# Wider operations, one y product a step and a new order in an S4 convolution with a GEGLU block

## The chip, the cores and the metric

The program runs on one core of one Trainium2 chip. The metric is the device time of one execution in microseconds (us). Five engines work side by side, each through its own instructions in order: TensorE (PE, matrix products), VectorE (DVE, elementwise), ScalarE (ACT, functions from a loaded table), GpSimd (POOL) and SyncE (SP). SP, ACT and POOL also issue the DMA transfers.

## The reference, cut to what matters

```python
h = layernorm(x) * (1 + ca) + sa            # x: 2048 tokens x 448 channels, N = 256 states
dt = exp(log_dt)                            # a value for each channel
P = exp((dt * (A_re + i A_im))[:, :, None] * l)          # l = 0 .. 2047
K = Re(einsum("dn,dnl,dn->dl", C, P, dt * B))            # a filter of 2048 taps for each channel
x = x + ga * (causal_conv(K, h) + h * Dskip)             # by FFT of length 4096
h = layernorm(x) * (1 + cb) + sb
x = x + gb * ((gelu(h @ w_gate) * (h @ w_up)) @ w_down)  # 448 -> 1792 -> 448
```

The six rows sa, ca, ga, sb, cb, gb are `silu(c) @ w_mod`.

## The kernel before, in words

**Filter.** The filter is made channel group by channel group: 56 steps of 8 channels. A tap index is split in two parts, l = 64 l1 + l2, so that a complex power is a product of an "x" table (32 values of l1) and a "y" table (64 values of l2), each a magnitude times a cosine or sine. For a step, PE multiplies the prepared exponents (tile `lt`) with constants (`ea`, `rd`) into PSUM tile `pg`; ACT takes exp of it for the magnitudes (`mx`, `my`; lines 775 and 793) and sine and cosine for the phases (tile `fg`; lines 811 to 830, in two ways: for the first 28 steps the cosine gets its own PSUM tile, for the last 28 it is made from an absolute value). DVE multiplies magnitude and phase: `tx` (line 855), and `ty` in three operations (`mults`, lines 859, 862, 863: cosine half, then the sine half in two pieces, one with a factor of -1). PE sums over the states: 64 small products into `kg` (`kgen`, line 886). After every second step `ktail` copies `kg` to `ke`, adds Dskip, multiplies with a small DFT matrix (line 911) and copies to `ako`.

**Preparation.** The exponents of a tile of 112 channels are made by `prep(t)`, t = 0 to 3: C times B as a complex product (lines 658 to 667), its size (square, log, square root by exp) and angle (reciprocal, arctan), each value then split in three bf16 pieces (`pieces`: cast, subtract, cast, subtract; lines 587, 643, 649) so that bf16 products on PE keep enough digits. Results go to DRAM (`lh_d`, line 696, `put0` and `put1`) and come back rearranged as `lt` (line 751), once per 7 steps and half: `lt0` for exp, `lt1` for the angles. Its inputs arrive in three DMAs (`q<-in_abc`, line 615). A block of ones for each tile (`lh_d<-in_k_one`, line 622) is copied by POOL's queue.

**Tokens.** Meanwhile the input is normalised with rows from `w_mod` (line 950), transformed (lines 1040, 1103), and stored; blocks of frequencies are then multiplied with those of the filter and transformed back (`k_fft`, lines 1194 to 1205, for the channel groups 0 to 159 and 160 to 319; `t_fft`, lines 1276 to 1300, for the last 128, after the last step). Copies from PSUM may run on ACT or DVE (`cp`, lines 585 and 587).

**GEGLU.** Four blocks of 512 tokens follow: convolution back (lines 1466, 1471), norm, transposes, gate and up products (line 1594), down products (lines 1663, 1694).

**Order.** The program is not written in its final order. Each piece of work is a task with a name, an engine (or a choice of two) with an assumed duration, the tasks that it needs and the buffers that it takes. `Plan.order` places tasks one by one: it takes the engine that could start earliest, and among that engine's tasks that could start within 0.25 us (ACT: 0.02 us) the one with the lowest number in the table `PRIO`. The order so found is what each engine then runs, in order. The assumed durations, a hop of 0.3 us between engines (`HOP`), 1.3 us for a table (`TABLE`) and 280 KB per us of DMA (`RATE`) enter that order alone; nothing of them is on the chip.

Of the kernel before, what the change touches and what calls it, by code (L numbers as in the profile page):

```python
# [37 lines left out]
WS = 256.0  # L38
PRIO = {
    "anc": (-1293.256, -3578.895, -353.961, -872.318, -460.437, -1921.377, -2404.991, -2215.805, 191.288, -32.981, -202.691,  # L40
        -2647.333, -1933.83, -670.792, -192.873, -616.144, -80.921, -1549.964, -2941.687, -671.342, -2001.879, -1132.111,
        -71.643, -27.945, -252.965, -1535.421, -769.379, -1539.333),
    "ang": (-63.859, -7.725, -30.71, 0.169, 7.925, 11.195, 9.268, 21.779, 22.824, 25.594, 26.183, 26.493, 28.144, 28.708,
# [5 lines left out]
    "c.ai": (-2663.528,),  # L49
    "c.ak": (171.218,),  # L50
    "c.au": (-4200.533,),
    "c.c": (-933.544,),
    "c.ea": (5422.27,),
    "c.id": (-147.248,),
    "c.ih": (1109.11,),
    "c.ld": (-3220.083,),
    "c.rd": (2966.135,),
    "co.adde": (-84.218, -1452.145, -2417.83, -1409.323),
    "co.addl": (-57.786, 676.69, 1533.586, 31.466),
    "co.addx": (-1428.076, -8.045, 2531.362, 3088.204, -2578.892, 2089.375, -473.92, 382.232, 1219.977, -537.482, 53.247,  # L60
        1140.208),
    "co.c2": (553.038, 3254.154, 1888.633, -595.169, 1726.527, -906.573, 4858.759, 40.493, -1400.834, 27.831, 1819.503,
        -161.366),
    "co.h": (336.967, 2645.855, 1868.777, -2126.118),
    "co.h2": (-650.973, 75.139, 637.166, -1259.465, -8.18, -1329.599, 13.947, -1333.575, 5413.552, -346.388, 3335.76, 1270.416),
    "co.l": (-2527.984, -675.661, 723.03, 3544.242),
    "co.l2": (1124.467, 1797.664, 1246.234, 626.032, 529.696, 1269.558, 529.646, -451.738, -1181.182, 2221.273, 450.372,
        434.525),
    "co.mme": (4028.037, 3822.614, -709.965, -3597.943),
    "co.mml": (-661.981, 33.929, 1870.772, -68.779),  # L70
    "co.mmx": (348.366, -620.465, 1977.413, 2997.574, -279.998, 3308.134, 630.569, 742.671, -398.692, -288.917, -47.372,
        2601.845),
    "co.n": (-637.705, -78.904, -2172.773, -124.152),
    "co.nx": (-1207.602, 1920.968, -700.888, 0.561, -1307.228, -3639.226, 373.628, -35.065, -24.718, 34.24, 1425.966, -6133.847),
    "co.rc": (1435.224, -2102.468, 1120.167, 435.885),
    "co.rcx": (864.192, -118.249, 3179.105),
    "co.rt": (-668.81, -40.146, 1435.174, -1099.33),
    "co.rtx": (-306.185, -80.314, 5310.55),
    "co.t": (-701.977, -362.858, 11.547, -251.511),
    "co.t2": (-1003.663, 677.507, 490.748, 1973.53, -67.147, -1774.919, -292.344, -677.791, 196.69, -3024.797, -183.214, 15.548),  # L80
    "cos": (47.809, 4338.677, -1916.389, -1985.479, 48.84, 450.345, -228.642, 1373.754, -1635.183, -2125.449, -2951.945,
        139.392, -590.217, -1488.189, -465.57, -115.397, -138.704, 2366.141, 654.971, 78.486, 63.259, -3501.827, 365.129,
        -594.75, 843.446, -2481.552, 3748.658, 338.746),
    "cos2": (-186.283, -458.553, -28.501, -1467.414, -186.383, 305.735, -4173.308, 2676.943, -903.314, -2645.906, -803.054,
        147.233, 61.493, -902.839, -698.019, 3.975, 96.182, 670.288, 4882.18, -890.924, -903.013, 1267.647, -38.519, 1684.391,
        654.047, -1006.703, 490.617, -217.831),
    "d.hi": (-16.935, -885.611, 1072.565, -1866.073, 565.92, -545.207, 277.832),
    "d.ld": (-1036.334, 594.218, -5342.563, -1512.808, 784.13, 1290.275, -992.387),
    "d.lo": (-1950.133, -1401.218, -2174.946, -390.7, -1260.169, -6.416, 1957.309),
    "d0": (-1079.999,),  # L90
    "dn": (-3573.259, -323.838, 1692.909, 1720.273),
    "dn.k0": (1759.554, 521.981, -3993.33),
    "dn.k2": (-1082.302, -1650.584, -6237.94),
    "dn.k3": (-388.073, 2717.888, 2751.692),
    "dn.r": (586.912, 103.145, 2224.364, -500.948),
# [430 lines left out]
def s4_geglu(ctx: ExitStack, tc: tile.TileContext, a: dict, out: bass.AP):  # L526
# [76 lines left out]
    def prep(t):  # L603
# [32 lines left out]
        def pieces(lb, q, get, deps, k, first):  # L636
# [5 lines left out]
            def p2():  # L642
                V.tensor_sub(get(), get(), lb.tile[:, q])
# [1249 lines left out]
```

## Time and profile before

| | us |
|---|---|
| median of 3 runs (823.48 to 825.14) | 824.81 |
| the profiled execution's own time | 822.29 |
| its span, first to last instruction | 820.5 |
| busy in the span: PE | 744.8 (91%) |
| DVE | 609.2 (74%) |
| ACT | 464.4 (57%) |

The span falls in four stages: to about 45 us the start, to 371 the 56 filter steps with the transforms beside them, to 420 the last transforms and the first normalisation, and to the end the GEGLU blocks. A busy time is the union over an engine's instructions; instructions of DVE and ACT that follow each other overlap a little in the trace, so that the distance of two starts is less than the duration of one. In a timeline row stand the start, the duration, the engine (with a q: its queue, for issues of DMAs), line, operation, output and input, and in brackets how long the engine sat idle before and what it then waited for.

### The profile page before, as it was taken

Reading aid. Unit: us, or ns where it says so; the run is one execution under the profiler, and the core shown is the slowest. Engines: PE = TensorE matmul, PEld = TensorE weight load, DVE = VectorE, ACT = ScalarE, POOL = GpSimd, SP = SyncE. Lnnn points to the kernel's source line nnn. Section 1 sums busy time; section 2 is a strip of 40 time slices with the busy share of each in tenths; the row PEclk is TensorE's granted clock in tenths of the full one; section 3 lists DMA queues with packets and bytes.
Section 4 is the critical chain, followed back from the end, with each engine's and each line's share of the span. In section 5 each row is a group of like instructions: output and inputs, shape, how many; then the busy total and the mean of one; then the engine's idle time right before and its main releaser. Section 6 shows DMA issues by size and latency. Waiting matters only on the chain.

```text
span 820.5 us, 19136 instructions
## 1 busy us (share of the span) xinstructions
PE 744.8 (91%) x8172; PEld 455.8 (56%) x8172; DVE 609.2 (74%) x1034; ACT 464.4 (57%) x610; POOL 11.1 (1%) x28
## 2 busy tenths in 40 slices
PE   0787788989899999988689999999999999999997
PEld 0333344443577766678566445444496445954477
DVE  5799999898989999996875783178884655744552
ACT  4598998999899999880245551034332233223320
POOL 1000000000000000001200000000000000000000
PEclk9879999999999999999879999999999999999999
DMA  9644459997967755989769641644416232012101
GB/s 266 161 147 138 116 145 246 282 261 234 221 198 223 224 160 165 295 276 279 242 224 310 234 158 63 162 150 139 135 53 185 77 127 96 24 68 90 45 13 35
DMA packets 92839, 136.78 MB, mean 167 GB/s; under 512 B 22672, under 2 KB 75184, under 8 KB 92754
## 3 DMA queue, kind: packets, MB, share of 16 engines
q1 hardware_dynamic: 86480, 131.02, 52.6%
q10 hardware_dynamic: 5458, 3.12, 1.3%
q8 instruction: 64, 1.05, 0.5%
q0 software_dynamic: 816, 1.42, 0.5%
q14 instruction: 21, 0.17, 0.1%
HBM read 100.42 MB, written 36.01 MB: 166 GB/s over the span
## 4 chain that ended last, share of the span: by engine, by line
PE 62%; ACT 14%; DVE 9%; DMA 8%; issue 5%; SPq 2%; ACTq 0%; DVEq 0%
PE pq L1594 30%; PE pq L1694 8%; PE pd L1663 4%; ACT fg L819 3%; PE kg L886 3%; DMA u_d<-so 2%; PE pg L806 2%; ACT my L793 2%; PE pq L1588 2%; PE pf L1205 2%; PE pf L1103 2%; PE pd L1694 1%; DMA fg<-in_w_mod 1%; DVE ty L859 1%; ACT fg L811 1%
## 5 line engine op out<-in xcount | busy, mean ns | idle before, releaser
L1594 PE MATMUL pq<-ht,wr 128*128 128x512 f16 (+1 forms) x1200 | 248.7, 365 | 0.0
L1594 PEld LDWEIGHTS <-wr 128*128 128x128 f16 x1200 | 114.4, 98 | 128.9 <-issue 12.3
L1608 DVE TENSOR_TENSOR fq<-ge,pq 128x512 f32<-128x512 f32 (+1 forms) x60 | 39.0, 651 | 83.4 <-PE pq L1594 58.5
L1601 ACT ACTIVATE ge<-pq 128x512 f32<-128x512 f32 (+1 forms) x60 | 34.0, 567 | 113.8 <-PE pq L1588 69.4
L1620 ACT ACTIVATE hh<-fq 128x1024 f16<-128x1024 f32 (+1 forms) x49 | 47.2, 964 | 59.9 <-DVE fq L1608 44.5
L886 PE MATMUL kg<-ty,tx 128*32 128x64 f32 x3584 | 63.6, 224 | 13.4 <-DVE ty L863 9.0
L886 PEld LDWEIGHTS kg<-ty,tx 128*32 128x32 f32 x3584 | 54.4, 112 | 32.7 <-DVE ty L863 14.0
L855 DVE TENSOR_TENSOR tx<-mx,fg 128x1024 f32<-128x1024 f32 x56 | 67.3, 1215 | 2.8 <-ACT fg L830 2.8
L1694 PE MATMUL pq<-d,hh 128*128 128x224 f16 x476 | 69.3, 259 | 0.0
L859 DVE TENSOR_TENSOR ty<-my,fg 128x1024 f32<-128x1024 f32 x56 | 67.9, 1216 | 1.7 <-ACT fg L823 1.7
L1694 PE MATMUL pq<-d,hlo 128*128 128x224 f16 x238 | 61.6, 259 | 0.0
L819 ACT ACTIVATE fg<-pg 128x1024 f32<-128x1024 f32 x56 | 57.7, 1032 | 3.5 <-issue 1.5
L793 ACT ACTIVATE my<-pg 128x1024 f32<-128x1024 f32 x56 | 55.9, 1037 | 5.6 <-PE pg L788 5.1
L1623 DVE TENSOR_TENSOR hlo<-fq,hh 128x1024 f16<-128x1024 f32 (+1 forms) x49 | 53.6, 1103 | 3.1 <-ACT hh L1620 3.1
L1694 PEld LDWEIGHTS <-hh 128*128 128x128 f16 x560 | 53.9, 98 | 0.8 <-issue 0.3
L1205 PE MATMUL pf<-q,fc 128*128 128x160 f32 x264 | 41.8, 307 | 0.2
L806 PEld LDWEIGHTS <-lt 64*128 64x128 bf16 x336 | 19.3, 94 | 40.0 <-issue 26.0
L1205 PEld LDWEIGHTS pf<-q,fc 128*128 128x128 f32 x264 | 36.6, 190 | 6.2 <-issue 3.4
L806 PE MATMUL pg<-ea,lt 64*128 64x512 bf16 x168 | 33.1, 387 | 6.7 <-ACT fg L819 5.2
L863 DVE TENSOR_TENSOR ty<-my,fg 128x512 f32<-128x512 f32 x56 | 38.2, 682 | 0.0
L862 DVE SCALAR_TENSOR_TENSOR ty<-my,fg 128x512 f32<-128x512 f32 x56 | 38.1, 681 | 0.0
L911 PE MATMUL kg<-ak,ke 128*64 128x128 f32 x448 | 30.6, 279 | 3.7 <-issue 2.0
(198 smaller groups left out, 1207.2 us busy)
## 6 DMA issues: line engine op xcount, KB each, us to landing
wr<-w_d SPq DMA_DIRECT2D x21, 896.0 KB, 4.6
fc<-in_k_fc SPq DMA_DIRECT2D x20, 576.0 KB, 5.2
u_d<-so SPq DMA_DIRECT2D x32, 224.0 KB, 4.5
w<-in_wgu SPq DMA_DIRECT2D x14, 512.0 KB, 4.1
ui<-u_d SPq DMA_DIRECT2D x10, 672.0 KB, 6.2
w_d<-wr SPq DMA_DIRECT2D x7, 896.0 KB, 7.1
fq<-in_wd SPq DMA_DIRECT2D x14, 448.0 KB, 3.8
us<-uo SPq DMA_DIRECT2D x22, 240.0 KB, 6.5
```

The costliest lines, as they stand in the source:

```text
L793: A.activation(yb.tile.rearrange("p a b c -> p (a b c)"), pb.tile, AF.Exp)
L806: T.matmul(pa[:, nh * 512:nh * 512 + 512], w, x, start=(k == 0), stop=(k == 2))
L819: A.activation(fb.tile[:, 0].rearrange("p x (n k) -> p n x k", n=2), pb.tile.rearrange("p (n x k) -> p n x k", n=2, x=2), AF.Sin, scale=TW ...
L855: V.tensor_mul(tx.tile, xb.tile[:, xm, None, :].to_broadcast([128, 2, 512]), fb.tile[:, :, 0])
L859: V.tensor_mul(ty.tile[:, 1], yb.tile, fy()[:, 1, :, None, :].to_broadcast([128, 16, 2, 32]))
L886: T.matmul(kg[32 * g:32 * g + 32, 2 * (s % 2) + q, :64], tx[:, r, nh, 4 * q + g], ty[:, r, nh, 4 * q + g], start=(r == 0 and nh == 0), sto ...
L1205: T.matmul(pz.tile[:, e % 32 - sl0], fc.tile[:, i, 1 + t], pp.tile[:, t, i], start=(t == 0 and e != 32), stop=(t == 1 and e != 0))
L1594: T.matmul(pb.tile[k][:, ts], wr.tile[:, 4 * lo + t, k, c0:c0 + 128], ht[:, m, ts], start=f % 2 == 0 and i == 0, stop=f % 2 == 1 and i == 9)
L1608: V.tensor_mul(to if half is None else to[:, half:half + 1], *src)
L1620: A.activation(hg.tile[0][:, cb, c], fq.tile[:, c], AF.Copy)
L1623: V.tensor_sub(hg.tile[1][:, cb, c], fq.tile[:, c], hg.tile[0][:, cb, c])
L1694: T.matmul(bank(k)[:, m], x[:, p, q[0], ts], w[:, p, q[1]], start=new and m == 0 and p == 0 and z == 0, skip_group_check=True, stop=i in ( ...
```

## The change

- **Preparation**: the inputs of a tile come in two DMAs (C and B together, then A) instead of three; the four products of C and B are one operation of 1024 columns; both values of a pair are split in pieces together (512 columns instead of 256 twice); small multiplications are folded elsewhere (`G1`).
- **Constants**: the blocks of ones of tiles 1 to 3 are read on SP's queue, each after its tile's inputs, instead of on POOL's at the start. `A_log_dt`, `c` and `A_Dskip` are laid out by the host so that a DMA reads whole rows.
- **y product**: signs move into the constants' phases (`ea`) and into the cosine's scale, and `ty` becomes one DVE operation of 2048 columns that needs sine, cosine and exp; `kgen` picks its operands from it by a stride. `my` is written in another layout.
- **Order**: assumed durations come from a table of measured ones (`COST`), hops from a table by pairs of engines, DMA is modelled by queue, PE's clock by a window; some kinds of tasks must keep their turn (`INTURN`); all numbers in `PRIO` are new.

The diff, cut:

```diff
+COST = {
+    ("anc", "PE", 0.76): 0.72, ("ang", "PE", 0.76): 0.72, ("bn", "DVE", 0.65): 0.73, ("c.ai", "SP", 0.42): 1.27,
...
 PRIO = {
-    "anc": (-1293.256, -3578.895, -353.961, -872.318, -460.437, -1921.377, -2404.991, -2215.805, 191.288, -32.981, -202.691,
...
 class Plan:
-    TABLE, HOP, STICK, BIAS, RATE = 1.3, 0.3, 103.13, -0.27, 280.0
+    TABLE, HOP, STICK, BIAS, RATE = 1.3, 0.3, 103.13, -0.27, 290.0
+    HOPD, HOPB, WINDOW, COLD, WARM, PHASE = 0.2, 0.16, 3.4133, 0.55, 0.83, 0.0
+    HOPS = {("PE", "ACT"): 0.18, ("PE", "DVE"): 0.18, ("ACT", "DVE"): 0.18, ("ACT", "PE"): 0.2, ("DVE", "ACT"): 0.115, ("DVE", "PE"): 0.14,
+            ("DVE", "DVE"): 0.12, ("ACT", "ACT"): 0.18, ("PE", "PE"): 0.0}
+    INTURN = ("ang", "tx", "tyc", "x.mm", "y.mm", "x.exp", "y.exp", "f.ut", "f.fc", "f.fwd", "f.inv", "lt0", "lt1", "ub.u", "ub.fc", "ub",
+              "kev", "ka", "t.fwd", "t.inv", "wr.ld")
...
     def prep(t):
-        for i in range(3):
-            loads.append(add("p.ld", {"SP" if i % 2 or t else "ACT": 0.42 if i % 2 or t else 0.1}, v0, lambda i=i: ld1(i), loads[:1],
-                             [b1, b2, b3] if i == 0 else [], [b1, b2, b3] if i else [], kb=253))
-
-        PAD[t] = add("pad", {"POOL": 1.0}, v0 + 0.5, lambda: P.dma_start(lh_d[t, :, :, 6:], a["k_one"][t]), loads, kb=229)
+        L0 = add("p.ld", {"SP" if t else "ACT": 0.42 if t else 0.1}, v0, lambda: ld1(0), (), us, (), kb=459)
+        PAD[t] = add("pad", {"SP": 0.7} if t else {"POOL": 1.0}, v0 + 0.5, lambda: (dma if t else P.dma_start)(lh_d[t, :, :, 6:], a["k_one"][t]), [L0], kb=300)
+        L1 = add("p.ld", {"SP": 0.42}, v0, lambda: ld1(1), [L0], (), us, kb=230)
...
-            V.tensor_mul(x, cr, br)
-            V.tensor_mul(t1, ci, bi)
-            V.tensor_sub(x, x, t1)
...
+            V.tensor_mul(b2.tile.rearrange("p (i j) n -> p i j n", i=2), b1.tile[:, :2, None].to_broadcast([DT, 2, 2, N]),
+                         b1.tile[:, None, 2:].to_broadcast([DT, 2, 2, N]))
...
     def mults(s):
-            V.tensor_mul(ty.tile[:, 1], yb.tile, fy()[:, 1, :, None, :].to_broadcast([128, 16, 2, 32]))
-
-        def fs():
-            V.scalar_tensor_tensor(ty.tile[:, 0, :, 0], yb.tile[:, :, 0], -1.0, fy()[:, 0], op0=OP.mult, op1=OP.mult)
-            V.tensor_mul(ty.tile[:, 0, :, 1], yb.tile[:, :, 1], fy()[:, 0])
+        def fy():
+            ty.tile = tab.tile([128, 2, 2, 512], FT, name="ty")
+            V.tensor_mul(ty.tile, yb.tile[:, :, None, :].to_broadcast([128, 2, 2, 512]),
+                         fb.tile[:, None, :, 1].to_broadcast([128, 2, 2, 512]))
         x = add("tx", {"DVE": 1.13}, s - 0.4, fx, [si, co, xt_], [tx], [fb, xb])
-        y = add("tyc", {"DVE": 1.13}, s - 0.4, fc_, [co, yt_], [ty], [fb, yb])
-        z = add("tys", {"DVE": 1.2}, s - 0.4, fs, [si, y], (), [fb, yb, ty])
-        return x, y, z
+        y = add("tyc", {"DVE": 2.21}, s - 0.4, fy, [si, co, yt_], [ty], [fb, yb])
+        return x, y
...
     def kgen(s, deps):
-                                     ty[:, r, nh, 4 * q + g], start=(r == 0 and nh == 0), stop=(r == 1 and nh == 1),
+                                     ty[:, 0:4:3, nh, 4 * q + g] if r else ty[:, 1:3, nh, 4 * q + g], start=(r == 0 and nh == 0), stop=(r == 1 and nh == 1),
```

Three places of the new order follow. The first is DVE's beginning. Before, the rows of tile 0's complex product (lines 658 to 667), behind a cast of the first piece:

```order
L587 CAST lh<-q 112x256
L658 TENSOR_TENSOR q<-q 112x256
L659 TENSOR_TENSOR q<-q 112x256
L660 TENSOR_TENSOR q<-q 112x256
L665 TENSOR_TENSOR q<-q 112x256
L666 TENSOR_TENSOR q<-q 112x256
L667 TENSOR_TENSOR q<-q 112x256
L643 TENSOR_TENSOR q<-q,lh 112x256
```

The same beginning now; L727 is the product of 1024 columns, L732 and L733 the two sums, L741 to L744 the size:

```order
L727 TENSOR_TENSOR q<-q 112x1024
L732 TENSOR_TENSOR q<-q 112x256
L733 TENSOR_TENSOR q<-q 112x256
L741 TENSOR_TENSOR q<-q 112x256
L742 TENSOR_SCALAR q<-q 112x256
L743 TENSOR_SCALAR q<-q 112x256
L744 TENSOR_SCALAR q<-q 112x256
```

Six operations became three, and the first piece's cast and subtraction no longer stand around them.

The second place is ACT at the end of tile 0's preparation. Before: L688 is the square root by exp, L716 the arctan, L967 copies a row of `w_mod`'s product from PSUM, L1017 the tokens' standard deviation, L696 the store `put0`:

```order
L688 ACTIVATE q<-q 112x256
L689 ACTIVATE q<-q,ld 112x256
L707 ACTIVATE q<-q 112x256
L585 ACTIVATE lh<-q 112x256
L967 ACTIVATE gs<-pf 128x448
L1017 ACT_TABLE_LOAD
L1017 ACTIVATE rs<-mv,small 128x8
L696 DMA lh_d<-lh 112x1536
L967 ACTIVATE rows<-pf 128x448
L716 ACT_TABLE_LOAD
L716 ACTIVATE q<-q 112x256
```

And now; L755 is the square root by exp, L765 the arctan, L1014 the copied row, L1064 the deviation, L780 the store:

```order
L755 ACTIVATE q<-q 112x256
L762 ACTIVATE q<-q,ld 112x256
L669 ACTIVATE lh<-q 112x2x256
L1014 ACTIVATE rows<-pf 128x448
L765 ACT_TABLE_LOAD
L765 ACTIVATE q<-q 112x256
L780 DMA lh_d<-lh 112x1536
L773 ACTIVATE q<-q 112x256
L1064 ACT_TABLE_LOAD
L1064 ACTIVATE rs<-mv,small 128x8
```

The arctan stands behind one row of `w_mod` instead of two, and ahead of the deviation and its table.

The third place is SP's queue as the filter steps end. Before: L1238 loads constants of the last transforms (`fg`, `my`), L1351 reads back the filtered tokens (`yi`), which waits for the stores of all earlier transforms:

```order
L1238 DMA my<-in_k_fc 128x384
L1238 DMA fg<-in_k_fc 128x1920 x2
L591 DMA ai<-in_k_ai 128x64
L1328 DMA x_5209<-in_A_u 128x1792
L591 DMA ident<-in_k_id 128x128
L1351 DMA yi<-y_67 64x2x640 x2
L1351 DMA yi<-y_68 64x2x640 x2
L591 DMA idenh<-in_k_ih 128x128
L1238 DMA my<-in_k_fc 128x768
```

And now, where L1285 loads those constants and L1398 reads back:

```order
L1285 DMA my<-in_k_fc 128x768
L1260 DMA y_68<-zo 128x3x160
L1285 DMA fg<-in_k_fc 128x1920
L1260 DMA y_68<-zo 128x2x160
L1295 DMA my<-us_66 128x128
L1285 DMA fg<-in_k_fc 128x1920
L675 DMA ident<-in_k_id 128x128
L675 DMA ai<-in_k_ai 128x64
L675 DMA idenh<-in_k_ih 128x128
L1375 DMA x_5054<-in_A_u 128x1792
L1398 DMA yi<-y_67 64x2x640 x2
L1398 DMA yi<-y_68 64x2x640 x2
```

The last load of `my` constants stood behind the read-back; now all of them stand ahead of it.

Counted in the order up to the last copy of `ako`, ACT has 3 table loads more (39 instead of 36), and of the work that may run on either engine DVE has 6 copies more of `ako`, 6 more of `so`, 3 more of `zo`, 2 more of the absolute values, and 1 copy of `uo` less. PE's work is the same.

More of the change, by code (lines that the diff above doesn't have):

```diff
@@ L371, in order @@
     def order(self):
-        free, table, dma, out = {}, None, 0.0, []
+        free, table, out = {}, None, []
+        dq = dict.fromkeys(("SP", "ACT", "POOL"), 0.0)
+        self.clock = [self.PHASE, 0.0, True]
         lane = {"SP": [-1e9] * 8, "POOL": [-1e9] * 8}
@@ L516, in constants @@
         "k_ak": ak.reshape(128, 256).astype(f),
-        "k_one": np.ones((4, 2, DT, 2, N), ml_dtypes.bfloat16),
+        "k_one": one,
         "k_ai": ai.reshape(128, 64).astype(f),
@@ L926, in ktail @@
         return t3
[L929 removed]
+    t_c = sp("c.c", -8.8, lambda: c_sb, lambda: a["c"], 2)
     def silu():
```

661 lines of the change are left out of this document (352 added, 309 removed), and 153 rows, old and new, of tables (COST, PRIO).

## The prediction

> **What bounds the kernel now.** I read the busy times by stage first, then the waits inside each stage. The columns are PE, weight loads, DVE, ACT and POOL busy (in us), PE's granted clock, and DMA.
>
> ```profile
> 0.00:45.00 45.00, 20.54 (x58) 9.28 (x59) 30.91 (x75) 23.64 (x36) 3.13 (x14) 0.87 0.78 217
> 45.00:371.00 326.00, 292.11 (x5268) 182.98 (x5267) 306.43 (x481) 301.55 (x385) 0.00 (x0) 0.98 0.71 208
> 371.00:420.00 49.00, 37.04 (x279) 32.67 (x280) 37.09 (x71) 8.97 (x14) 7.94 (x14) 0.83 0.77 236
> 420.00:820.50 400.50, 395.09 (x2571) 230.83 (x2569) 234.77 (x410) 130.23 (x176) 0.00 (x0) 1.00 0.37 119
> ```
>
> The last stage is PE work without gaps (395.09 of 400.50 us at full clock) and the change leaves PE's work alone, so it gives and takes nothing there. In the 326 us of filter steps DVE is busy for 306.43, ACT for 301.55 and PE for 292.11: three engines nearly full, DVE the fullest. A saving there counts only if DVE does less or idles less, and ACT has not 5 us to spare. DVE idles 45.00 - 30.91 = 14.1 us in the start and 326.00 - 306.43 = 19.6 in the steps. The whole change can hardly win more than these 34 us and what it takes out of DVE's work.
>
> How evenly the steps run is seen from two pieces of the stage:
>
> ```profile
> 100.00:150.00 50.00, 43.73 (x757) 22.88 (x754) 46.09 (x84) 45.02 (x62) 0.00 (x0) 0.97 0.75 203
> 250.00:300.00 50.00, 48.76 (x899) 36.46 (x900) 48.36 (x70) 48.00 (x55) 0.00 (x0) 1.00 0.66 194
> ```
>
> DVE idles 3.9 us in the first and 1.64 in the second. At the second's rate the stage would idle 1.64 x 326 / 50 = 10.7 us instead of 19.6.
>
> **The y product.** The timeline of DVE shows operations of the step back to back:
>
> ```profile
> 217.15 1.21 DVE L859 TENSOR_TENSOR ty<-my,fg 128x1024 f32<-128x1024 f32 x1
> 218.28 0.68 DVE L862 SCALAR_TENSOR_TENSOR ty<-my,fg 128x512 f32<-128x512 f32 x1
> 218.88 0.68 DVE L863 TENSOR_TENSOR ty<-my,fg 128x512 f32<-128x512 f32 x1
> 219.49 0.68 DVE L862 SCALAR_TENSOR_TENSOR ty<-my,fg 128x512 f32<-128x512 f32 x1
> ```
>
> What an operation takes from the engine is the distance of the starts: 1.13 us for 1024 columns, 0.60 for 512. The three now take 1.13 + 0.60 + 0.61 = 2.34. One of 2048 columns, on the same slope of 0.53 for 512, takes 1.13 + 2 x 0.53 = 2.19. That is 0.15 less, and 56 x 0.15 = 8.4 us in all. An operation of this width is not shown. Its strides may cost something, up to what merging saves, so the gain is 0 to 8.4; a loss I exclude, since the three pieces read broadcast and strided operands too and lie on one slope. I take the whole slope for that reason.
>
> [...]
>
> ```profile
> L859 DVE TENSOR_TENSOR ty<-my,fg 128x1024 f32<-128x1024 f32 x56 | 67.9, 1216 | 1.7 <-ACT fg L823 1.7
> L863 DVE TENSOR_TENSOR ty<-my,fg 128x512 f32<-128x512 f32 x56 | 38.2, 682 | 0.0
> L862 DVE SCALAR_TENSOR_TENSOR ty<-my,fg 128x512 f32<-128x512 f32 x56 | 38.1, 681 | 0.0
> ```
>
> By durations, 1216 + 682 + 681 = 2579 ns become 1216 + 2 x (1216 - 682) = 2284, 295 less, 16.5 us over 56 steps. The starts say that half of this fixed part already lies under the operation before. [...]
>
> **The preparation and what moved to DVE.** For the rest I count the orders up to the last `ako` copy and use distances of starts; the rows not yet shown:
>
> ```profile
> 41.84 0.42 DVE L658 TENSOR_TENSOR q<-q 112x256 f32<-112x256 f32 x1
> 42.18 0.42 DVE L659 TENSOR_TENSOR q<-q 112x256 f32<-112x256 f32 x1
> 14.30 0.28 DVE L684 TENSOR_SCALAR q<-q 112x256 f32<-112x256 f32 x1
> 14.50 0.28 DVE L685 TENSOR_SCALAR q<-q 112x256 f32<-112x256 f32 x1
> 204.86 0.61 DVE L587 COPY uo<-pf 128x448 f32<-128x448 f32 x1
> 205.40 0.41 DVE L649 TENSOR_TENSOR lh<-q,lh 112x256 bf16<-112x256 f32 x1
> ```
>
> - Products and differences: 48 operations of 256 columns go (0.34 each, 16.3 us); 16 of 512 (0.60) and 4 of 1024 (1.13) come, 14.1 us. Saved: 2.2.
> - Casts: 27 of 256 at about 0.21 (the single-source rows), 5.7 us, become 11 of 512 at about 0.34 (estimate: 0.21 and half of what columns cost a two-source operation), 3.7. Saved: 2.0.
> - Copies that come over from ACT: 6 `ako` of 512 columns (0.60), 5 more of 448 (`so` 6, `uo` -1; 0.54), 3 `zo` (0.57), 2 absolute values (1.13): 3.6 + 2.7 + 1.7 + 2.3 = 10.3 more.
>
> DVE's work thus changes by -8.4 - 2.2 - 2.0 + 10.3 = -2.3 us. The widening is mostly spent on taking work from ACT. ACT in turn loses those copies and 17 operations of 256 columns, gets 9 of 512, and three table loads more:
>
> ```profile
> 212.75 0.38 ACT L585 ACTIVATE ke<-kg 128x252 f32<-128x252 f32 x1
> 213.16 1.28 ACT L793 ACT_TABLE_LOAD   x1
> 214.45 2.85 ACT L793 ACTIVATE my<-pg 128x1024 f32<-128x1024 f32 x3
> 242.39 0.59 ACT L585 ACTIVATE ako<-kg 128x512 f32<-128x512 f32 x1
> 242.87 1.02 ACT L811 ACTIVATE fg<-pg 128x1024 f32<-128x1024 f32 x1
> ```
>
> A table load takes 1.29 us from start to start, with nothing before or behind it: 3.9 for three. A 512-column copy takes 0.48, a 1024-column function 2.85 / 3 = 0.95 at most. The 14 copies and 2 absolute values are at most 14 x 0.48 + 2 x 0.95 = 8.6 less. The preparation is 17 x 0.41 (at most, by the `ke` row) less 9 x 0.48, so 0 to 2.7 less. ACT's net is -4.7 to -7.4, say -6. [...]
>
> **The start.** The first sines of the steps come late, because tile 0's preparation does:
>
> ```profile
> 0.75 0.93 ACTq L615 DMA_DIRECT2D q<-in_abc  x2
> 4.90 0.49 SPq L615 DMA_DIRECT2D q<-in_abc  x1
> 5.45 0.49 ACT L676 ACTIVATE q<-q,dts__102 112x256 f32<-112x256 f32 x1
> 9.59 0.42 DVE L659 TENSOR_TENSOR q<-q 112x256 f32<-112x256 f32 x1 [2.99 <-DMA q<-in_abc]
> 21.97 0.42 DVE L714 TENSOR_TENSOR q<-q 112x256 f32<-112x256 f32 x1
> 24.25 0.55 ACT L967 ACTIVATE gs<-pf 128x448 f32<-128x448 f32 x1 [4.01 <-PE pf L950]
> 29.11 0.42 ACT L716 ACTIVATE q<-q 112x256 f32<-112x256 f32 x1
> 34.90 0.33 ACTq L696 DMA_DIRECT2D lh_d<-lh  x1
> 51.70 1.02 ACT L819 ACTIVATE fg<-pg 128x1024 f32<-128x1024 f32 x1
> ```
>
> The product waits to 9.59 for the load that SP issues at 4.90, behind others. In the new order all of C and B is one load on ACT's queue at 0.75; the loads issued there were used by 5.45, so the product can begin near 5.5, 4 us earlier. The angle's slope is ready at 22.4 but its arctan waits to 29.11, behind two rows of `w_mod` and the deviation's table. Now it stands behind one row: even if that row came as late as 24.25, the arctan would end by 24.25 + 0.55 + 1.28 + 0.42 = 26.5 instead of 29.5; with the row's load earlier in the queue, about 22. So `put1` should leave 3 to 8 us before 34.90, and the first sine come near 46 instead of 51.70.
>
> This is not a gain of 6 us in the end: the steps are bound by DVE, and DVE was busy for 30.91 of the first 45 us with work that stays. What counts is its idle time. Waiting to 5.5 instead of 9.59 less the 0.71 us done before saves 3.4; new short waits (for ACT between the wider operations, and for the last row of `w_mod`) give some back. I take 14.1 - 12 = 2 us, between 0 (all given back) and 8.6 (only the first 5.5 us idle). The three blocks of ones leave the start's DMA and go to SP's queue behind their tile's load; the first of them is needed with the second tile, 14 steps later.
>
> **Idle time of DVE in the steps.** The stage's groups name what is waited for: `zo` and `tx` wait for PE and ACT, and the largest wait of PE is for DVE's last y piece.
>
> ```profile
> L855 DVE TENSOR_TENSOR tx<-mx,fg 128x1024 f32<-128x1024 f32 x56 | 67.3, 1215 | 2.8 <-ACT fg L830 2.8
> L886 PE MATMUL kg<-ty,tx 128*32 128x64 f32 x3584 | 63.6, 224 | 13.4 <-DVE ty L863 9.0 <-DVE tx L855 2.9 <-issue 1.3
> ```
>
> They are many short waits. An order placed with durations nearer to those of the rows (an `ako` copy on ACT was assumed at 0.52 and takes 0.48) shortens some: 0 to 19.6 - 10.7 = 8.9 us. ACT with 6 less to do is less often the one waited for. I take 6, nearer to the stretch from 250 to 300, which shows what the same step can do. That part is a choice, not a count.
>
> **After the steps.** The chain there, in order of time:
>
> ```profile
> 382.94 3.97 DMA y<-zo
> 386.93 5.47 DMA my<-in_k_fc
> 393.15 7.16 PE pf L1292 x64
> 400.33 0.61 ACT lh L585
> 400.96 3.19 DMA y<-lh
> ```
>
> The last constants land at 392.4 because their load stands on SP behind the read-back. Now it is issued ahead. But PE idled only 49.0 - 37.0 = 12 us in the whole stage, and the trip through DRAM behind 400.33 stays. I take 1.5 us, between -1 and 5.
>
> **The sum.** Against the profiled execution (822.29; its span is 820.5): -2.3 - 2 - 6 - 1.5 = -11.8, so 810.5. The median of the runs, 824.81, is 2.5 above the profiled one; I predict 813.0 for it. Its own range takes the ends that lie together: 805 to 819.
>
> **Rivals.**
>
> - *The head start is eaten* (20%): DVE idles in the steps as before, and only work and start count, -4.3: 820.5. For it: three engines over 89% full leave an order little to win. Against it: the piece from 250 to 300.
> - *The wide product blocks DVE's queue* (12%), slower. DVE works in order; a copy that PE's PSUM buffers wait for (28 `ke` sums, 12 `ako`, 14 `so`, 12 `uo`, 12 `zo`: 78) may now stand behind 2.19 us instead of 1.13. Half the difference is 0.53 us; y products fill 56 x 2.19 / 326 = 38% of the time, so 78 x 0.38 x 0.53 = 15.7 us if all of it shows. With the 4.3 of the first rival and no gain from the order that is +11.4: 836. It decides once over a quarter of those waits (4.3 of 15.7) is exposed and the order gains nothing. For it: PE already waits 9.0 us for y pieces. Against it: two buffers of `kg` and `pf`.
> - *No change* (6%): the strides of the new product cost what merging saves (8.4), and the start's gain makes up for DVE's extra copies: 824.8.
> [...]
> - The forecast has 55%.
>
> **How the numbers follow.** A measurement tells this kernel from no change at about 0.2%, 1.65 us. Forecast, head start and fixed part are faster: 0.55 + 0.20 + 0.07 = 0.82; no change is 0.06, slower 0.12. For 8 in 10 the range leaves out the slow rival and the ends: 803 to 823.
>
> **What would show it.** Right: the product of 1024 columns starts near 5.5, the first sine near 46; y products start 2.19 apart; the filter steps end near 361 instead of 371; DVE idles under 15 us in the steps; the last stage is 400 us as now. Wrong: y products over 2.35; waits of PE for `ke` and `pf` grown to over 10 us; the steps' end less than 4 us earlier.

## The result, and the profile after

| | before | after |
|---|---|---|
| median of the runs, us | 824.97 (823.48 to 825.14) | 832.47 (830.47 to 833.72) |
| profiled execution, us | 822.29 | 831.4 |
| its span | 820.5 | 829.6 |

The ratio is 1.0093 (95% interval 1.0066 to 1.0119): 7.5 us slower, where 11.8 us less was forecast. The median before is now over four runs; the 824.81 of the prediction was over three of them. The four stages of the changed kernel, in the columns of the first view of the prediction:

```profile
0.00:45.00 45.00, 20.10 (x70) 9.87 (x71) 31.74 (x64) 25.70 (x38) 1.48 (x11) 0.96 0.80 210
45.00:371.00 326.00, 288.57 (x5096) 179.26 (x5092) 298.62 (x344) 293.05 (x358) 0.00 (x0) 0.95 0.69 204
371.00:420.00 49.00, 36.97 (x411) 32.93 (x409) 35.35 (x62) 9.53 (x16) 8.41 (x15) 0.90 0.81 245
420.00:829.60 409.60, 402.83 (x2602) 236.11 (x2602) 243.27 (x430) 131.00 (x176) 0.00 (x0) 0.99 0.37 119
```

The boundaries no longer fit: in the same 326 us all three engines do less, because the steps run on past 371. The timeline of the changed kernel gives the landmarks: the first product, `put1`, the first sine, two y products, the last `ako` copy, the first gate product.

```profile
5.94 1.23 DVE L727 TENSOR_TENSOR q<-q 112x1024 f32<-112x1024 f32 x1 [5.02 <-DMA q<-in_abc]
28.97 0.49 ACTq L780 DMA_DIRECT2D lh_d<-lh  x1
43.27 1.02 ACT L873 ACTIVATE fg<-pg 128x1024 f32<-128x1024 f32 x1
95.94 4.48 DVE L910 TENSOR_TENSOR ty<-my,fg 128x2048 f32<-128x2048 f32 x2
381.53 0.69 DVE L671 COPY ako<-kg 128x512 f32<-128x512 f32 x1 [2.40 <-PE kg L958]
428.71 0.82 PE L1641 MATMUL pq<-ht,wr 128*128 128x256 f16 x3
```

Before, the last two came at these times:

```profile
374.05 0.69 DVE L587 COPY ako<-kg 128x512 f32<-128x512 f32 x1 [2.56 <-PE kg L911]
419.71 0.72 PE L1594 MATMUL pq<-ht,wr 128*128 128x256 f16 x5
```

The head start came as forecast, and more: the first sine runs at 43.27 instead of 51.70. The last copy of the steps is 7.5 us later, so the head start of 8.4 us and 7.5 more, 16 us in all, were lost on the way; another 1.5 are lost behind the steps. From the first gate product to the end of the span nothing changed (400.8 us before, 400.9 now).

Two y products take 4.48 us, so their starts lie 4.48 - 2.29 = 2.19 apart, exactly as forecast. DVE's work to the last `ako` copy, in both:

```profile
0.00:374.05 374.05, 313.74 (x5340) 193.25 (x5340) 337.83 (x556) 325.19 (x420) 3.13 (x14) 0.96 0.72 210
0.00:381.53 381.53, 316.22 (x5340) 195.37 (x5340) 337.26 (x417) 321.28 (x399) 1.48 (x11) 0.96 0.71 208
```

For DVE it is the same work in 7.5 us more, so what grew is its waiting. The waits of PE between 45 and 375 us (total, times, longest), the largest before, then some after. The two lists are cut, and the steps of the changed kernel run on past 375:

```profile
PE kg L886 <- DVE ty L863: 9.0, 10, 2.4
PE pg L806 <- ACT fg L819: 5.2, 8, 1.5
```

```profile
PE pg L842 <- ACT my L847: 4.5, 9, 0.9
...
PE pg L842 <- ACT mx L829: 3.4, 4, 1.5
PE pg L823 <- ACT mx L829: 3.2, 4, 1.5
PE pf L1252 <- issue: 2.8, 1, 2.8
...
PE pg L860 <- ACT my L847: 2.3, 4, 0.8
```

PE hardly waits for the y product any more (1.3 us between 40 and 380 us). It waits for ACT instead, whose exp (`mx`, `my`) still reads the PSUM tiles `pg` that PE would write.

### The profile page after: what moved, and what is told of

It is laid out like the page before. It is cut to its first block, busy times and chain, and to the rows that moved or that the text cites. A ratio compares the mean times of both kernels' runs of the same rounds, so it can differ in the third digit from the quotient of the medians.

```text
span 829.6 us, 18963 instructions
## 1 busy us (share of the span) xinstructions
PE 748.5 (90%) x8172; PEld 458.2 (55%) x8172; DVE 609.0 (73%) x897; ACT 459.3 (55%) x586; POOL 9.9 (1%) x26
## 4 chain that ended last, share of the span: by engine, by line
PE 48%; issue 48%; DMA 1%; DVE 1%; POOL 1%; ACT 0%; ACTq 0%; POOLq 0%
PE pq L1641 29%; PE pq L1741 8%; PE pd L1710 4%; PE pq L1635 2%; PE pd L1741 1%; PE pd L1513 1%; PE pt L1565 1%; PE pt L1588 1%; DMA yi<-zo 1%; DMA yi<-y 0%; PE pd L1518 0%; DMA y<-zo 0%; PE pt L1567 0%; POOL yi L1421 0%; PE pd L1801 0%
## 5 line engine op out<-in xcount | busy, mean ns | idle before, releaser
L910 DVE TENSOR_TENSOR ty<-my,fg 128x2048 f32<-128x2048 f32 x56 | 127.4, 2285 | 2.0 <-PE kg L933 1.2
L860 PE MATMUL pg<-ea,lt 64*128 64x512 bf16 x168 | 34.8, 399 | 8.4 <-ACT fg L873 4.7
L860 PE MATMUL pg<-ea,rd 64*128 64x512 bf16 x168 | 35.0, 394 | 1.1 <-issue 1.1
L842 PE MATMUL pg<-ea,lt 64*128 64x512 bf16 x112 | 22.5, 410 | 13.8 <-ACT my L847 4.5
L860 PE MATMUL pg<-rd,lt 64*128 64x512 bf16 x168 | 34.8, 394 | 0.0
```

The lines of the kernel that those rows point to most:

```text
L860: T.matmul(pa[:, nh * 512:nh * 512 + 512], w, x, start=(k == 0), stop=(k == 2))
L910: V.tensor_mul(ty.tile, yb.tile[:, :, None, :].to_broadcast([128, 2, 2, 512]), fb.tile[:, None, :, 1].to_broadcast([128, 2, 2, 512]))
```

## The experiments

**Operations and order apart.** An order can be recorded: each task's place and engine is written down, and the other kernel's tasks are placed by it. That gives the operations of one kernel in the order of the other.

```diff
     def order(self):
+            rank[t] = RANK[t.n].split()[seen[t.n]]
...
+            t = min((t for t in ready if self.slot(t) is not None), key=lambda t: float(rank[t][1:]))
```

> All of the new operations (wide preparation, constants, one y product a step), but every engine runs its instructions in the order of the kernel before; the y product stands where the last third of the old one stood. Theory 'order' (the new operations gain what was forecast, and the new order loses it in the steps): 824.8 less 8.4 for the y products and some 4 for the preparation, about 812 (808 to 816). Theory 'wide product' (a product of 2.2 us delays what stands behind it in DVE's queue): 830 or more, as slow as the changed kernel.

> The opposite corner: the operations of the kernel before, in the order of the changed kernel; all three pieces of the y product stand where the one product stands. Theory 'order': 832.5 plus what the operations are worth, 840 to 848. Theory 'wide product': 820 to 826, since no product is wide and the order is free of blame.

| | old order | new order |
|---|---|---|
| old operations | 824.8 | 845.8; ratio 1.0268 (1.0241 to 1.0295) |
| new operations | 821.7; 0.9966 (0.9948 to 0.9985) | 832.5; 1.0093 (1.0066 to 1.0119) |

Theory "wide product" falls: with the wide product in the old order the kernel is faster than before, and without it in the new order it is 21 us slower. The new order costs 832.5 - 821.7 = 10.8 us (7.7 to 13.2 by the two intervals). But "order" is only half right, since it had the operations worth 12 to 13 us and they gained 3.1. In the new order the operations look worth 13.3 us (845.8 to 832.5). There, though, the many small operations of the old preparation stand where the few wide ones were placed, so that this figure is not the worth of the operations alone.

**The merge alone**, in both orders:

```diff
-            V.tensor_mul(ty.tile, yb.tile[:, :, None, :].to_broadcast([128, 2, 2, 512]),
-                         fb.tile[:, None, :, 1].to_broadcast([128, 2, 2, 512]))
+            V.tensor_mul(ty.tile[:, :, 1], yb.tile, fb.tile[:, 1, None, 1].to_broadcast([128, 2, 512]))
+            for h in range(2):
+                V.tensor_mul(ty.tile[:, h, 0], yb.tile[:, h], fb.tile[:, 0, 1])
```

> The changed kernel in its own order, but the y product is cut in three at its place (1024, 512 and 512 columns). DVE has 8.4 us more to do. Theory 'order': 836 to 841, the 8.4 us or half of them. Theory 'wide product': the three pieces stand at the same place in the queue, so that only the total counts: also slower, by the same; faster than 832.5 only if the wide form itself is slow. It sizes the merge inside the new order.

> New preparation and constants in the order of the kernel before, with the y product in three pieces where they stood. It differs from the kernel before in the preparation and the constants alone, and from the run of all new operations in that order in the merge alone. Theory 'order': 820 to 823, and the merge worth 8 us more. Theory 'wide product': 820 to 823 as well, and the merge costs instead: this one is then the fastest of the four.

833.6 in the new order (1.0097, 1.0075 to 1.0119) and 823.0 in the old one (0.9972, 0.9955 to 0.9990). By the medians the merge is worth 1.2 us in each, not 8.4, and the intervals don't tell that from nothing. Yet DVE's work did shrink. To the last `ako` copy, in the old order, in three pieces and in one:

```profile
0.00:379.10 379.10, 317.60 (x5340) 196.01 (x5340) 334.14 (x516) 322.46 (x408) 1.48 (x11) 0.95 0.72 212
0.00:371.60 371.60, 311.92 (x5340) 192.94 (x5340) 326.98 (x404) 322.33 (x408) 1.49 (x11) 0.97 0.73 213
```

334.14 - 326.98 = 7.2 us less DVE work bought 1.2 us in the medians. (The two profiled executions differ by more than that; they lie at the two ends of their runs.)

**Who ends the steps?** If not DVE, then who? Each cut takes some 30 us of work from one engine, in the old order with the new operations; the filter is another one in all four. The edits, cut to their main lines:

```diff
-            V.tensor_mul(tx.tile, xb.tile[:, xm, None, :].to_broadcast([128, 2, 512]), fb.tile[:, :, 0])
+            V.tensor_mul(tx.tile[:, 0], xb.tile[:, xm], fb.tile[:, 0, 0])
...
-            A.activation(fb.tile[:, 1], fb.tile[:, 1], AF.Sin, scale=-TWO_PI, bias=halfpi)
+            A.activation(fb.tile[:, 1, 0], fb.tile[:, 1, 0], AF.Sin, scale=-TWO_PI, bias=halfpi)
...
-                for r in range(2):
+                for r in range(1):
                     for nh in range(2):
```

> New operations in the order of the kernel before; the x product makes the sine half alone (512 columns instead of 1024) and PE reads it twice, so the filter is another one. DVE has 56 x 0.53 = 30 us less to do in the steps. Theory 'DVE ends the steps': 821.7 falls by 20 to 30, to 792 to 802. Theory 'three engines in a chain' (each step's end hangs on PE, ACT and DVE in turn, and DVE is not the last): less than 8, to 814 to 821.

> New operations in the order of the kernel before; the cosine is made for the x half alone (512 columns instead of 1024) and the y product takes the sine twice, so the filter is another one. ACT has 56 x 0.48 = 27 us less to do. Theory 'ACT ends the steps': 821.7 falls by 15 to 27, to 795 to 807. Theory 'DVE ends the steps': less than 5. Theory 'chain': some 5 to 12, and about as much as for the half x product.

> New operations in the order of the kernel before; PE sums over half of the products only (32 small ones a step instead of 64), so the filter is another one. PE has half of 63.6 us less to do, 32 us. Theory 'PE ends the second half of the steps' (there PE idles 1 to 5 us in 70): some 14 to 20 us come off, 821.7 to 802 to 808; in the first half, where it idles more, little. Theory 'chain or order' (no engine ends the steps, the places in the order do): less than 6, as for the half x product (3.1) and the half cosine (3.6).

> New operations in the order of the kernel before, with both of the earlier cuts: half of the x product and half of the cosine, so DVE has 30 us and ACT 27 us less to do, and the filter is another one. Theory 'PE ends the second half, the loads the middle': the gain stays small, 4 to 9 us (the two single gains together are 6.7), 813 to 818. Theory 'DVE and ACT in turn' (each takes over as soon as the other is lightened): 15 to 25 us, 797 to 807.

| cut | us | ratio to before | beyond the uncut kernel's 3.1 |
|---|---|---|---|
| x product (DVE -30) | 818.6 | 0.9938 (0.9911 to 0.9965) | 3.5 |
| cosine (ACT -27) | 818.1 | 0.9913 (0.9877 to 0.9950) | 4.0 |
| sums (PE -32) | 819.6 | 0.9915 (0.9884 to 0.9947) | 2.5 |
| x product and cosine | 814.3 | 0.9871 (0.9821 to 0.9921) | 7.9 |

The last column is the kernel before in the same runs, less the cut one, less 3.1. By the ratios it would be 2.3, 4.4, 4.2 and 7.8; each interval is 2 to 4 us wide to either side. No engine by itself ends the steps: whichever is relieved of some 30 us, 2 to 4 come off, and 8 of 57 for two. Every theory that priced the relief of one engine at 14 us or more falls. The run with two cuts came out as the theory of PE and the loads had it (4 to 9 off), but the cut of PE itself brought 2.1 us, where that theory had 14 to 20. The profile shows a part of the reason, once the steps are cut in pieces that belong together. These stretches run from the 28th y product to the 42nd, fourteen steps; in this order: the kernel before, the uncut kernel, the cut of the x product, of the cosine, of the sums.

```profile
224.70:294.10 69.40, 68.20 (x1346) 51.25 (x1342) 65.22 (x93) 67.79 (x80) 0.00 (x0) 1.00 0.70 208
...
221.70:292.70 71.00, 68.34 (x1348) 51.35 (x1344) 63.85 (x66) 68.33 (x80) 0.00 (x0) 1.00 0.69 203
...
223.10:292.60 69.50, 68.34 (x1350) 51.44 (x1346) 57.53 (x65) 67.88 (x80) 0.00 (x0) 1.00 0.70 208
...
221.60:292.10 70.50, 68.17 (x1347) 51.20 (x1344) 63.80 (x65) 63.07 (x80) 0.00 (x0) 1.00 0.68 205
...
224.90:294.90 70.00, 63.02 (x900) 45.80 (x897) 63.59 (x66) 68.29 (x80) 0.00 (x0) 1.00 0.70 205
```

Before, PE idled 1.2 of 69.4 us here and ACT 1.6; DVE, with 4.2, was the idlest of the three. Taking 6 to 8 us from DVE leaves 69.5 us, because PE still has 68.3 to do. Taking 5 from PE leaves 70.0, because ACT has 68.3. In this stretch the cuts of one engine took 0.5 to 1.5 us from the uncut kernel's 71.0, no more than the idle time of the next (2.7).

At the beginning it is otherwise. Before, and with the new operations in the old order, from the first y product to the 14th:

```profile
54.80:130.30 75.50, 58.92 (x1096) 32.69 (x1095) 74.09 (x127) 68.49 (x95) 0.00 (x0) 0.93 0.45 130
...
54.20:126.70 72.50, 57.56 (x1084) 32.38 (x1080) 70.45 (x89) 66.17 (x91) 0.00 (x0) 0.93 0.44 132
```

There DVE is busy for 74.09 of 75.50 us, and the 3.6 us of work that it lost turned into 3.0 us of time. From the 42nd y product to the 56th DVE is the fullest too, and 1.9 us less work went with 1.7 us less time:

```profile
294.10:365.10 71.00, 65.62 (x1300) 49.53 (x1301) 67.21 (x95) 65.40 (x76) 0.00 (x0) 1.00 0.73 233
...
292.70:362.00 69.30, 64.46 (x1298) 48.86 (x1298) 65.29 (x66) 64.57 (x76) 0.00 (x0) 1.00 0.75 239
```

But the idle time of the next engine is a ceiling, not the amount. The cut of the x product, from the first y product to the 14th:

```profile
56.60:128.90 72.30, 60.74 (x1086) 34.34 (x1085) 64.86 (x89) 66.08 (x89) 0.00 (x0) 0.88 0.45 134
```

DVE has 5.6 us less to do than in the uncut kernel, ACT idles 6.2 us, and the stretch is 0.2 us shorter. What holds the steps there, no run shows. From the 14th to the 28th all three idle 7 to 8 us of 94, in the kernel before:

```profile
130.30:224.70 94.40, 86.70 (x1342) 41.98 (x1340) 86.49 (x149) 87.44 (x120) 0.00 (x0) 1.00 0.92 256
```

The DMA share is 0.92 in this stretch against 0.45 and 0.70 in the others. That transfers hold these steps is a reading of the row; no run cut a transfer.

**What in the new order costs 10.8 us?** First guess: the 10.3 us of copies that went from ACT to DVE, or the work that the early first sine pushed back. Each of two runs undoes one of these changes in the recorded order.

> The changed kernel in its own order, but every copy and absolute value that may run on ACT or DVE runs on the engine that it had before: DVE gets rid of the 10.3 us of copies that came over. Theory 'copies' (what the new order loses is this work on DVE): 832.5 less 10, about 822. Theory 'places' (the order loses by where the operations stand, whatever their engine): 828 to 838.

> New operations in the order of the kernel before, except that the first 111 tasks (up to the first y product) come as in the changed kernel: the first sine runs near 43 instead of 48.8, because six exp of y and two transforms of tokens are put off until behind it. Theory 'head start': the 5.5 us are kept, 816. Theory 'put off': the same work is only done later, 821 to 823 as in the old order throughout.

With the copies on their old engines the new order takes 850.4 (1.0308, 1.0265 to 1.0352): 18 us worse, not 10 better. The run changes more than the 10.3 us: it moves 45 operations from DVE to ACT and 31 from ACT to DVE, each at its place in the new order. So it does not price the copies; it suggests that places and engines belong together. The first 111 tasks of the new order in front of the old one give 828.1 (1.0048, 1.0019 to 1.0078), 6 us slower than the old order throughout, although the first sine comes 5.7 us earlier. ACT's timeline, first of the old order throughout, then of this run, shows what the early sine is paid with:

```profile
46.50 1.02 ACT L847 ACTIVATE my<-pg 128x1024 f32<-128x1024 f32 x1 [0.40 <-PE pg L842]
47.54 1.28 ACT L873 ACT_TABLE_LOAD   x1
48.84 1.02 ACT L873 ACTIVATE fg<-pg 128x1024 f32<-128x1024 f32 x1
```

```profile
43.18 1.02 ACT L873 ACTIVATE fg<-pg 128x1024 f32<-128x1024 f32 x1
...
47.55 1.28 ACT L847 ACT_TABLE_LOAD   x1
51.55 1.02 ACT L847 ACTIVATE my<-pg 128x1024 f32<-128x1024 f32 x1 [2.72 <-PE pg L842]
52.59 1.28 ACT L884 ACT_TABLE_LOAD   x1
...
54.92 1.28 ACT L847 ACT_TABLE_LOAD   x1
56.22 4.69 ACT L847 ACTIVATE my<-pg 128x1024 f32<-128x1024 f32 x5
60.92 1.28 ACT L873 ACT_TABLE_LOAD   x1
```

Six exp of y, which the old order does ahead of the first sine, now stand behind it, with table loads between and a wait for PE. The splice itself makes part of these loads, so this shows that an early sine is worth nothing by itself, not what it costs in the new order. In this splice even the first y product comes late, at 55.9 us; it comes at 54.2 in the old order and at 46.5 in the changed kernel.

**Splices** at the first y product, at step 13, at step 27, and the complement:

> New operations; up to the first y product in the order of the kernel before (the six exp of y done ahead of it), everything behind in the new order. Theory 'start' (what the new order loses comes mainly from putting those exp behind the first sine, as the reverse cut showed with 6.4 us): 832.5 less 6, about 826. Theory 'spread' (the loss lies in the places all along the steps): 830 to 833.

> New operations; old order up to the y product of step 13, new order behind. Theory 'start': as the run before, about 826, since what follows costs little. Theory 'second half' (28 steps in which all three engines are nearly full, and PE idles more in the new order): 828 to 831. Theory 'spread': 829.

> New operations; old order up to the y product of step 27, new order behind. Theory 'start': 821 to 823, as in the old order throughout. Theory 'second half': the 10 us by which steps 27 to 55 were longer in the profiles come back in part, 826 to 830. Theory 'spread': 826.

> New operations; new order up to the y product of step 27, old order behind: the complement of the run before. Theory 'start': 828, the 6.4 us and nothing more. Theory 'second half': 822 to 825. The two complements should add up to the 10.8 us between the orders, if the halves are independent.

836.4 (1.0131), 831.4 (1.0088), 832.0 (1.0077) and 836.0 (1.0122). "Start" falls: the old start in front of the new order makes it slower, not 6 us faster. The second and third come nearest to "second half", but the complement, for which that theory had 822 to 825, is 14 us slower. By itself the new first half costs 14.3 us against the old order throughout, the new second half 10.3, and both together 10.8: the parts are not independent, and a seam, the place where the two orders meet, has a price of its own. The trace of the last run shows such a price. Its seam is behind the 28th y product:

```profile
223.84 2.29 DVE L910 TENSOR_TENSOR ty<-my,fg 128x2048 f32<-128x2048 f32 x1
...
231.39 1.97 PE L1241 MATMUL pf<-ako,fc 128*128 128x160 f32 x6 [4.77 <-DMA fc<-in_k_fc]
...
242.29 2.29 DVE L910 TENSOR_TENSOR ty<-my,fg 128x2048 f32<-128x2048 f32 x1 [1.83 <-ACT fg L873]
```

The 28th and the 29th y product are 18.5 us apart, 6.4 in the old order throughout. So the seam alone takes 12 us more, with a wait for a load in it, in an execution of 830.4 us (8.7 above the old order's median); the new first half in front of it costs little by itself. So the times of the splices can't say where this order loses; the traces say more. The changed kernel, between its 1st, 14th, 28th, 42nd and 56th y product:

```profile
46.50:131.30 84.80, 67.06 (x1108) 35.76 (x1105) 80.29 (x108) 77.73 (x97) 0.00 (x0) 0.84 0.45 130
131.30:224.70 93.40, 85.72 (x1368) 41.89 (x1368) 81.50 (x99) 82.78 (x111) 0.00 (x0) 0.99 0.88 255
224.70:298.90 74.20, 70.47 (x1334) 51.97 (x1324) 70.08 (x73) 67.98 (x78) 0.00 (x0) 1.00 0.71 207
298.90:375.10 76.20, 67.58 (x1380) 52.28 (x1380) 69.45 (x71) 63.94 (x74) 0.00 (x0) 1.00 0.74 236
```

| stretch, us | before | new operations, old order | changed kernel |
|---|---|---|---|
| start to 1st y product | 54.8 | 54.2 | 46.5 |
| 1st to 14th | 75.5 | 72.5 | 84.8 |
| 14th to 28th | 94.4 | 95.0 | 93.4 |
| 28th to 42nd | 69.4 | 71.0 | 74.2 |
| 42nd to 56th | 71.0 | 69.3 | 76.2 |
| 56th to last `ako` copy | 9.0 | 9.6 | 6.4 |

The head start of 8 us is gone by the 14th y product; up to there ACT does 11.6 us more work behind the first y product, and DVE 9.8 more, than in the old order. At the 28th the kernel before and the changed one are level (224.7 in both). From the 28th y product to the last `ako` copy the changed kernel then takes 156.8 us, the old order 149.9. That recurs: 154 to 161 us in the seven traces with the new order there, whatever stands ahead, and 149 to 154 in the kernel before and in the five others that make the whole filter with the old order there and no seam at the 28th. In these traces some 6 to 7 us of the loss therefore come with the order of the last 28 steps. Between the 28th and the 56th y product DVE has 10.4 us more to do than in the old order and idles as long (10.9 and 11.2 us); PE idles 12.3 instead of 7.5 us, and ACT 18.5 instead of 7.4. That the work on DVE ends these steps is a reading that fits these rows; against it, the three-piece product in the new order gave DVE more work too, and its median is only 1.2 us higher. No run took work from DVE there and left the places alone.

**The granted clock.** In the changed kernel PE's granted clock between 45 and 130 us is lower (0.84 against 0.93 in the old order). In pieces of 1 us its trace shows stretches at 0.50, from 84 to 89 us for one, with 1.00 from 90 to 94; they come to 30 us in the steps. With the new operations in the old order, rows of 10 us from 20 to 130 us give 20 us at half clock, where the expectation has 24. Additional products from constants ahead of each token product were to hold it up. Their 12 us are an estimate: in the last stage of the kernel before, at a clock of 1.00, 1040 products of 512 columns took 230.3 us, by which 64 of 448 take 12.4.

```diff
+                    for _ in range(2):
+                        T.matmul(pbs[h].tile, ea[:, :128], ea[:, :D], start=True, stop=True)
```

> New operations in the order of the kernel before; ahead of each of the 16 token products PE makes four products of 448 columns from constants into the same PSUM tiles, which are overwritten: 12 us of PE work at full clock, none of it used, where PE waits for DVE. Theory 'clock' (windows at half clock in the first 14 steps cost time): the half-clock windows between 20 and 130 us (24 us now) mostly go, and 821.7 becomes 817 to 820. Theory 'idle PE costs nothing there': the additional work only stands in the way, 822 to 828.

> The changed kernel with the same additional products ahead of the token products. It has 30 us of half clock in the steps, most of it before 134. Theory 'clock': a third to a half of its loss against the old order comes back, 832.5 to 826 to 829. Theory 'idle PE costs nothing there': 832 to 838.

825.3 (1.0004, 0.9979 to 1.0029) and 834.0 (1.0106, 1.0070 to 1.0141): measured against the kernel before of the same runs, 3.1 and 1.3 us slower than without the additional products. The 1.3 lies inside the intervals. The third column from the end is the clock. The rows are the new operations in the old order, the same with additional products, the changed kernel, the same with them:

```profile
45.00:130.00 85.00, 68.39 (x1199) 37.64 (x1196) 80.94 (x105) 76.88 (x103) 0.00 (x0) 0.93 0.49 146
...
45.00:130.00 85.00, 71.97 (x1184) 36.26 (x1185) 79.34 (x107) 77.17 (x103) 0.00 (x0) 0.96 0.47 139
...
45.00:130.00 85.00, 67.37 (x1084) 35.47 (x1083) 80.43 (x107) 77.49 (x97) 0.00 (x0) 0.84 0.43 127
...
45.00:130.00 85.00, 72.80 (x1096) 35.01 (x1096) 76.14 (x102) 73.33 (x89) 0.00 (x0) 0.90 0.38 112
```

The clock rose, 0.93 to 0.96 and 0.84 to 0.90, and the time did not fall. This remedy fails. What a higher clock would be worth without the additional work, these runs don't show.

**Early heads.** The last theory: operations stand at the head of a queue before what they wait for, while the next one is ready. Such an operation changes places with the next: the 16th copy `zo`, for one, goes behind the y product that has place 1085. In short form:

```diff
-rank["f.z"][15] = "D1082"
+rank["f.z"][15] = "D1085.4"
```

> The changed kernel; at 12 places (7 on DVE, 5 on ACT) where by its trace an operation stood at the head of the queue waiting 0.3 to 2.4 us while the next one was ready, the two change places. These waits come to 4.1 us on DVE and 5.3 on ACT. Theory 'early heads' (the new order loses because it expects PE's products and loads earlier than they come): 832.5 less 3 to 6, 827 to 829. Theory 'chain' (the waits only move to the next place): 831 to 834.

> New operations in the order of the kernel before, with the same repair by its own trace: 8 places (4 on DVE with 2.6 us of waits, 4 on ACT with 4.3). Theory 'early heads': 821.7 less 2 to 4, 818 to 820, and the fastest version so far. Theory 'chain': 820.5 to 823.

831.5 (1.0093, 1.0056 to 1.0130) and 824.4 (0.9978, 0.9949 to 1.0007). Against the kernel before of the same runs the new order gained 1.5 us in the medians and the old one lost 2, both inside the intervals. "Early heads" falls in both. The time of the new order fits "chain", by which the waits only move on; the old order came out above the range of either theory.

What stays open: which property of the new order costs the 10.8 us. It isn't the wide product. Taking back all engine choices at once, filling PE for a higher clock, and exchanging single heads do not repair it. That the order as a whole does it is shown, and the traces put the larger part of it into the last 28 steps; why is not. The fastest version found that makes the right filter is the new operations in the old order, 821.7.

## Why the prediction was wrong

In the prediction's own terms the two profiled executions add up as follows. DVE's work changed by -0.6 us (forecast -2.3), its idle time in the first 45 us by -0.8 (14.1 to 13.3; forecast -2), its idle time from there to the last `ako` copy by +8.9 (22.1 to 31.0; forecast -6), and the stretch behind by +1.5 (forecast -1.5): +9.0, and the spans differ by 9.1. The step that failed is above all the idle time in the steps, and under it the view that DVE bounds them.

- **Idle time in the steps**, -6: wrong in sign, and the largest error. A better-measured table of durations was taken as a reason for a better order, "a choice, not a count". The new order cost 10.8 us instead. Up to the last `ako` copy DVE idled 36.2 us in the kernel before and 44.6 with the new operations in the old order, where its work fell by 10.9 us: most of the work saved became waiting. In the changed kernel it idles 44.3 us, so the new order won none of that back, and its 10.3 us of copies came on top as work.
- **What bounds the kernel.** This step failed too. The prediction saw three engines nearly full, but called DVE the fullest from sums over 326 us (306, 302, 292) and took every saving on DVE at full worth. In the row for 250 to 300 that it quotes itself, PE had the least idle time (1.24 us of 50; DVE 1.64, ACT 2.00), so that less work on DVE there mostly lengthens DVE's own waits.
- **The y product.** The price was right (2.19), so was the slope, and strides cost nothing: 2285 ns measured for 2048 columns, 2284 on the slope of the pieces. Its worth was wrong: 1.2 us against 8.4. In the kernel before DVE is the fullest engine in the first 14 steps and the last 14 only, so that half of the 8.4 was the most to expect by the stretches. Neither 8.4 nor the 16.5 by durations came out as time here.
- **Preparation and copies.** As work they were counted well. DVE's work fell from 337.83 to 334.14 by the preparation (-3.7; -4.2 forecast) and to 326.98 by the merge (-7.2; -8.4 forecast), and with the new order's copies it is 337.26 (+10.3, as forecast). Preparation, constants and the earlier start brought 1.8 us of time together, the merge 1.2; what the copies cost in time no run isolates.
- **The start.** The product (5.94), `put1` (28.97) and the first sine (43.27) came about where they were forecast. With the new operations alone the first sine moved by 2.9 us, from 51.70 to 48.84; the rest is exp put off behind it, and by the 14th y product nothing was left of the head start (131.3 us, 130.3 before).
- **After the steps**, -1.5: became +1.5 (47.2 us from the last `ako` copy to the gate products, 45.7 before). No run isolates it.
- **The rivals.** "The head start is eaten" has a time (820.5) near that of the new operations in the old order (821.7), but by luck: it had DVE's idle time unchanged and 2.3 us less work, and there it was 8.4 us more idle time and 10.9 us less work. "The wide product blocks DVE's queue" had the sign but not the cause: in three pieces at the same place the kernel is no faster (833.6), and PE's waits for the `ke` sums fell from 1.7 to 0.4 us. The fixed part, 0.07 in the sum of the chances, would take the 16.5 us by durations as time; no run shows that: the y products start 2.19 us apart, DVE's work fell by 7.2 us and the time by 1.2. "No change" falls with the interval of the result.

## What to carry to other kernels

Before pricing a saving on the fullest engine, cut the stage where the work changes and look at the idle time of the next engines in each piece: in the stretches measured here a saving brought no more than that, and once far less (5.6 us of work, 0.2 of time). Where three engines are nearly full, some 30 us taken from one of them gave 2 to 4. When a change brings both new operations and a new order, record one order and run the operations in both; here the gain and the loss were hidden in one number.

## What the runs showed of the hardware

The same program took different times at different mean granted clocks of PE. Of twelve runs of the new operations in the old order the ends were 816.8 us of span at a mean clock of 0.977 and 824.0 at 0.964. The clock lost is 0.023 x 816.8 = 18.8 us and 0.036 x 824.0 = 29.7; 10.9 us more of it went with 7.2 us more time, and a line through all twelve has a slope of 0.58. So about half of the lost clock showed as time here, and over the 23 runs of the kernel before that ran beside them the slope is 0.36. One reason why it is not all of it may be that PE waits for others in part of that time anyway; no run isolates it.

A table load took 1.28 us in every row shown, also right behind a function (one that ends at 47.52 us, the load at 47.54). And one profiled execution lay 5.7 us off its kernel's median (837.1 against 831.4, the splice at step 13), more than most of the single causes sought here.
